# A gated product in two passes over its weights, with block pairs as the moved operand

## The chip, the cores and the metric

The kernel runs on one core of one Trainium2 chip, in one launch. The metric is the device time of the launch in microseconds, the median of several runs.

## The reference

```python
x = retention(q, k, v)                      # 4608 tokens x 512
h = x @ w_in                                # 512 -> 2048
g = h * cos(h)
x = g @ w_out                               # 2048 -> 512     (the stage that the change rewrites: "wo")
h = max(max(x @ w1, x @ w2), x @ w3)        # 512 -> 768      ("b")
out = h @ w_out2                            # 768 -> 512
```

## The kernel before

The 4608 tokens are 9 blocks of 512 (`NBLK`, `NB`); blocks 1 to 8 also make four pairs (`NDUO`), and block 0 stands alone. Every matrix product is cut into quarters and done with seven half-size products (`P_A11`, `P_A12`, `P_A22`, `P_S1` to `P_S4`), whose operands are quarters, differences and sums of differences of the quarters. Each operand is held as a high and a low part, so that a half-size product of one piece is three matmuls: low weight by high operand, high by high, high by low. The high part is a cast on ScalarE, the low part a subtraction on VectorE.

The stages follow each other on TensorE: attention, first gated product (`wi`, in two phases of nine blocks), second gated product (`wo`), the three products of `b`, the last product `o`. The order of the work is written by hand: TensorE's code advances a counter, one slot for the matmuls of one half-size product, and `at(n, fn)` puts `fn` (a cast, a difference, a load, a store) n slots later. Each engine does its instructions in the order in which they are written. DMAs are issued by SyncE (SP), in order too.

In `wo`, `phase_out` goes block by block; in a block, over 4 groups of two weight tiles; in a group, over the seven products, 12 matmuls of 256 moved columns each (`product_out`, L870). All eight weight tiles of `wo` are resident, and seven PSUM banks keep a block's sums over its 4 groups. `build_out` makes a group's operands: load of four quarters in two DMAs (`k_g<-gq`), four differences (L375, of which two operands `ta` and `tb` come), casts (L830, L838) and low parts (L834 for one quarter, L843 for pairs of 128x1024). `finish_out` adds the banks up and stores a block's result (`x2p<-o_wo`).

The gate `h*cos(h)` is done in `gate` (L510 to L523), and stored to `gq` in rows of 4 KB for each partition. Weights are prepared during earlier stages: `background` reads, converts and splits one weight tile of a later stage (L185 to L229; its sum on GpSimd is L196) and stores it; `take` loads such a tile whole (1792 KB); `take_split` loads the plain weights and splits them in place (L203 to L229). The weight tiles 4 to 7 of `wo` are split by `take_split` at the end of the first product and in the first 15 slots of `wo`.

Of the kernel before, what the change touches and what calls it, by code (L numbers as in the profile page):

```python
# [11 lines left out]
F32R = mybir.dt.float32r  # L12
# [8 lines left out]
NB = 512  # L21
# [80 lines left out]
def retention_ffn(ctx: ExitStack, tc: tile.TileContext, att, w_in, w_out, w123, w_out2, cst, out):  # L102
# [4 lines left out]
    xpool = ctx.enter_context(tc.tile_pool(name="xpool", bufs=22))  # L107
# [326 lines left out]
    def last_product(own_slot=True):  # L434

        g = pending.pop()
        if "last" in g:
            g["last"]()
            tick()
            return  # L440
        g["go"](g["d"], P_A22, False)
        nc.scalar.activation(g["s1"][:, 0], g["d"][:, : g["n"]], AF.Copy, scale=g["scale"])
        g["done"](g, 1)
        if own_slot:
            tick()

    def group_in(ws, xs, name, done, where, duo=False, tile=None, scale=1.0, seeded=None):
        n = NB if duo else HB * len(ws)
        g = {"name": name, "n": n, "done": done, "at": where, "scale": scale}
        tile = tile or x4  # L450

        def copy(dst, b):
            nc.scalar.activation(dst, b[:, :n], AF.Copy, scale=scale)  # L453

        def plus(dst, b):
            if scale == 1.0:
                nc.vector.tensor_tensor(out=dst, in0=dst, in1=b[:, :n], op=ALU.add)  # L457
            else:
                nc.vector.scalar_tensor_tensor(
                    out=dst, in0=b[:, :n], scalar=scale, in1=dst, op0=ALU.mult, op1=ALU.add  # L460
# [349 lines left out]
    for i, (n, m) in enumerate(((-13, -2), (-11, 0), (-9, 7), (-7, 12))):  # L810
        take_split("wo", 4 + i, endB + n, endB + n + 4, *(endB + m + k for k in (0, 1, 1, 2)))

    def gate_half(g, half):
        j, k = g["at"]
        gate(g[f"s{half}"], f"{g['name']}_{half}", gq[j][k][:, 2 * half : 2 * half + 2], 0 if half else 3)


    OUT_ORDER = (P_A11, P_A12, P_S4, P_S2, P_A22, P_S3, P_S1)

    def build_out(name, n, src, offs, load, t1=(0, nc.gpsimd), t3=(0, nc.gpsimd), last=3):  # L820

        o = {"name": name, "n": n}
        pairs = ((P_A12, P_S4, "k2"), (P_S2, P_A22, "tb"), (P_S1, P_S3, "ta"))

        def first_high():
            x = o["x"] = x4(f"x_{name}", [2, n], F32R)
            nc.scalar.copy(x[:, 0], o["k1"][:, 0])  # L830
            o[P_A11] = (x[:, 0], x[:, 1])

        def first_low():
            nc.vector.tensor_tensor(out=o["x"][:, 1], in0=o["k1"][:, 0], in1=f32(o["x"][:, 0]), op=ALU.subtract)  # L834

        def pair_high(k):
            h = o["h", k] = x4(f"h{k}_{name}", [2, n], F32R)
            nc.scalar.copy(h, o[pairs[k][2]])  # L838

        def pair_low(k):  # L840
            h = o["h", k]
            lo = x4(f"l{k}_{name}", [2, n], F32R)
            nc.vector.tensor_tensor(out=lo, in0=o[pairs[k][2]], in1=f32(h), op=ALU.subtract)  # L843
            for i in range(2):
                o[pairs[k][i]] = (h[:, i], lo[:, i])

        at(load, lambda: load_quarters(o, src))
        at(offs[t1[0]], lambda: difference(o, 1, t1[1]))
        at(offs[t3[0]], lambda: difference(o, 3, t3[1]))
        at(offs[0], first_high)  # L850
        at(offs[1], first_low)
        at(offs[1], lambda: pair_high(0))
        at(offs[2], lambda: difference(o, 2, nc.vector))
        at(offs[2], lambda: pair_low(0))
        at(offs[2], lambda: difference(o, 4, nc.vector))
        at(offs[3], lambda: pair_high(1))
        at(offs[last], lambda: pair_high(2))
        at(offs[4], lambda: pair_low(1))
        at(offs[5], lambda: pair_low(2))
        return o  # L860

    def product_out(b, ws, product, x, n, first, last):
        for mt in range(2):
            m = slice(mt * 128, mt * 128 + 128)
            for p, w in enumerate(ws):
                c = slice(p * HB, p * HB + HB)
                wh, wl = w[product][:, 0, m], w[product][:, 1, m]
                xh, xl = x[product][0][:, c], x[product][1][:, c]
                for i, (a, v) in enumerate(((wl, xh), (wh, xh), (wh, xl))):
                    nc.tensor.matmul(  # L870
                        b[:, mt * HB : (mt + 1) * HB],
                        a,
                        v,
                        start=first and mt == 0 and p == 0 and i == 0,
                        stop=last and p == len(ws) - 1 and i == 2,
                        skip_group_check=True,
                    )
# [533 lines left out]
```

## Time and profile before

| what | value |
| --- | --- |
| median of 3 runs | 1441.6 us (1440.66 to 1441.9) |
| the profiled execution's own time | 1442.28 us |
| its span in the trace | 1440.5 us |
| granted TensorE clock over the span | 0.995 |
| TensorE busy | 98% |
| VectorE / ScalarE / GpSimd busy | 81% / 54% / 12% |

The difference of 1.8 us between the time and the span lies outside what the trace shows. Busy shares are means over stages with different limits; for `wo` the windows of that stage count, which runs from 543.6 to 915.5 us.

### The profile page before, as it was taken

Reading aid. Unit: us, or ns where it says so; the run is one execution under the profiler, and the core shown is the slowest. Engines: PE = TensorE matmul, PEld = TensorE weight load, DVE = VectorE, ACT = ScalarE, POOL = GpSimd, SP = SyncE. Lnnn points to the kernel's source line nnn. Section 1 sums busy time; section 2 is a strip of 40 time slices with the busy share of each in tenths; the row PEclk is TensorE's granted clock in tenths of the full one; section 3 lists DMA queues with packets and bytes.
Section 4 is the critical chain, followed back from the end, with each engine's and each line's share of the span. In section 5 each row is a group of like instructions: output and inputs, shape, how many; then the busy total and the mean of one; then the engine's idle time right before and its main releaser. Section 6 shows DMA issues by size and latency. Waiting matters only on the chain.

```text
span 1440.5 us, 26312 instructions
## 1 busy us (share of the span) xinstructions
PE 1413.1 (98%) x10492; PEld 1299.3 (90%) x10492; DVE 1160.7 (81%) x1649; ACT 778.1 (54%) x1259; POOL 178.1 (12%) x128
## 2 busy tenths in 40 slices
PE   7999999999999998999999999999999999999998
PEld 5899999998999998999999999988888888888887
DVE  7988888779787779999999998668576667868875
ACT  4666666667787776444444443344344434534543
POOL 3343443331022000000000000000000000000000
PEclk9999999999999999999999999999999999999999
DMA  9779989868999985365565567723433294435633
GB/s 359 254 280 321 317 285 342 299 259 298 359 387 351 339 288 170 126 224 199 189 210 195 189 227 289 303 74 125 142 129 125 86 372 176 156 132 167 227 117 117
DMA packets 95034, 331.52 MB, mean 230 GB/s; under 512 B 9408, under 2 KB 17600, under 8 KB 88768
## 3 DMA queue, kind: packets, MB, share of 16 engines
q1 hardware_dynamic: 94912, 329.85, 64.4%
q8 instruction: 82, 1.34, 0.4%
q14 instruction: 40, 0.33, 0.1%
HBM read 197.69 MB, written 132.12 MB: 229 GB/s over the span
## 4 chain that ended last, share of the span: by engine, by line
PE 81%; DVE 3%; DMA 3%; issue 1%; ACT 0%; SPq 0%; DVEq 0%; ACTq 0%
PE wo L870 23%; PE d_e L428 13%; PE d_a L406 11%; PE b_e L428 7%; PE b_a L406 6%; PE d_u L1272 5%; PE a_e L428 3%; PE sums L406 3%; PE b_u L1272 2%; PE d_b L406 2%; PE sc L567 1%; PE po L626 1%; PE a_u L1272 1%; DMA k_z<-x2q 1%; PE state L610 1%; PE po L638 1%
## 5 line engine op out<-in xcount | busy, mean ns | idle before, releaser
L870 PE MATMUL wo<-h_g,w_wo 128*128 128x256 f32 x1728 | 313.3, 283 | 0.0
L870 PEld LDWEIGHTS wo<-h_g,w_wo 128*128 128x128 f32 x1728 | 269.9, 192 | 0.0
L870 PE MATMUL wo<-l_g,w_wo 128*128 128x256 f32 x864 | 245.4, 284 | 4.6 <-DVE l_g L843 4.5
L870 PEld LDWEIGHTS wo<-l_g,w_wo 128*128 128x128 f32 x864 | 166.1, 192 | 5.6 <-DVE l_g L843 5.4
L406 PE MATMUL d_a<-x_x,w_wi 128*128 128x256 f32 x864 | 122.5, 290 | 1.0 <-DVE x_x L383 1.0
L523 DVE SCALAR_TENSOR_TENSOR s_a<-t_a,s_a 128x1024 f32<-128x1024 f32 x72 | 93.6, 1300 | 31.1 <-ACT t_a L520 31.0
L428 PE MATMUL d_e<-h_e,w_b 128*128 128x512 f32 x432 | 115.5, 389 | 0.0
L406 PE MATMUL d_a<-x_y,w_wi 128*128 128x256 f32 x864 | 112.6, 287 | 2.5 <-DMA x_y<-xs 2.1
L406 PEld LDWEIGHTS d_a<-x_x,w_wi 128*128 128x128 f32 x864 | 108.3, 190 | 6.7 <-issue 1.9
L838 ACT CAST h_g<-tb_g 128x1024 fp32r<-128x1024 f32 x36 | 37.8, 1051 | 141.1 <-DVE tb_g L375 141.1
L406 PEld LDWEIGHTS d_a<-x_y,w_wi 128*128 128x128 f32 x864 | 108.9, 196 | 2.9 <-ACT ar_wo L184 2.3
L514 DVE SCALAR_TENSOR_TENSOR t_a<-s_a,t_a 128x1024 f32<-128x1024 f32 x72 | 96.0, 1334 | 18.0 <-ACT t_a L510 17.7
L453 ACT ACTIVATE ext<-d_e 128x512 f32<-128x512 f32 x72 | 43.0, 597 | 116.6 <-PE d_e L428 116.3
L428 PEld LDWEIGHTS d_e<-h_e,w_b 128*128 128x128 f32 x432 | 81.0, 188 | 16.8
L196 POOL TENSOR_TENSOR fa_b<-raw_b 128x512 uint32<-128x512 uint32 x18 | 22.5, 1250 | 537.5 <-DVE raw_b L190 506.8
L520 ACT ACTIVATE t_a<-t_a 128x1024 f32<-128x1024 f32 x72 | 76.0, 1055 | 21.9 <-DVE t_a L514 21.8
L594 ACT COPY u<-state 128x128 f32<-128x128 f32 x128 | 31.4, 264 | 96.6 <-PE state L610 96.2
L510 ACT ACTIVATE t_a<-s_a 128x1024 int32<-128x1024 f32 x72 | 76.1, 1056 | 1.3 <-PE d_a L406 0.4
L457 DVE TENSOR_TENSOR ext<-ext,b_e 128x512 f32<-128x512 f32 x36 | 24.7, 686 | 57.5 <-PE b_e L428 57.5
L428 PE MATMUL d_e<-l_e,w_b 128*128 128x512 f32 x216 | 66.5, 389 | 0.0
L406 PE MATMUL b_a<-x_x,w_wi 128*128 128x256 f32 x432 | 61.1, 289 | 0.6 <-DVE u L576 0.6
L406 PE MATMUL b_a<-x_y,w_wi 128*128 128x256 f32 x432 | 58.0, 283 | 1.7 <-DMA x_y<-xs 1.4
(268 smaller groups left out, 3248.4 us busy)
## 6 DMA issues: line engine op xcount, KB each, us to landing
u<-att SPq DMA_DIRECT2D x36, 1024.0 KB, 7.4
gq<-s_a SPq DMA_DIRECT2D x72, 512.0 KB, 5.4
k_g<-gq SPq DMA_DIRECT2D x72, 512.0 KB, 6.0
xs<-x_x SPq DMA_DIRECT2D x63, 512.0 KB, 5.5
x_y<-xs SPq DMA_DIRECT2D x63, 512.0 KB, 7.3
w_b<-st_b SPq DMA_DIRECT2D x9, 1792.0 KB, 11.3
st_b<-p_b SPq DMA_DIRECT2D x27, 512.0 KB, 5.1
mqp<-ext SPq DMA_DIRECT2D x24, 512.0 KB, 3.1
```

The source lines that it names most:

```text
L406: nc.tensor.matmul(h[:, p * HB : (p + 1) * HB], a, b, start=first and p == 0 and i == 0, stop=i == len(terms) - 1, skip_group_check=True,)
L428: nc.tensor.matmul(dst, a, b, start=first and i == 0, stop=i == len(terms) - 1, skip_group_check=True)
L453: nc.scalar.activation(dst, b[:, :n], AF.Copy, scale=scale)
L457: nc.vector.tensor_tensor(out=dst, in0=dst, in1=b[:, :n], op=ALU.add)
L510: nc.scalar.activation(st["t"], s, AF.Copy, bias=0.25)
L514: nc.vector.scalar_tensor_tensor(out=r, in0=s, scalar=MOST_TURNS, in1=st["t"], op0=ALU.min, op1=ALU.subtract)
L520: nc.scalar.activation(r, r, AF.Sin, scale=TURN, bias=HALF_PI)
L523: nc.vector.scalar_tensor_tensor(out=s, in0=f32(st["t"]), scalar=-1.0, in1=s, op0=ALU.max, op1=ALU.mult)
L594: nc.scalar.copy(um, st)
L838: nc.scalar.copy(h, o[pairs[k][2]])
L870: nc.tensor.matmul(b[:, mt * HB : (mt + 1) * HB], a, v, start=first and mt == 0 and p == 0 and i == 0, stop=last and p == len(ws) - 1 and ...
L1272: nc.tensor.matmul(dst, a, v, start=first and p == 0 and i == 0 and (wide or mt == 0), stop=p == 2 and i == 2, skip_group_check=True,)
```

## The change: two passes, block pairs, and accumulating DMAs

`wo` is done in two passes (`half`) over the weights: pass 0 with tiles 0 to 3, pass 1 with tiles 4 to 7. The unit of work is a block pair (`m` 0 to 3) or block 0 alone (`m` None). Pass 0 goes 0, None, 1, 2, 3, pass 1 goes None, 0, 1, 2, 3. A unit does the seven products over both groups of its half; a slot is 12 matmuls of one group and one product. A pair's matmul moves 512 columns as a view of 2 x 256; block 0's moves 256. `P_A22` of a unit is done inside the next unit, after its `P_S2` (`pending`).

A unit's operands are built from quarters of 128x1024 (`WO_STEPS`): seven casts, seven low parts, and three differences on VectorE for each group; the fourth, q0+q2, is formed by a DMA from GpSimd's queue that adds the quarter from DRAM onto the tile in SBUF (`add`). The gate is stored with its sign turned, into rows of 2 KB for each block of a pair (`gqp`). Results of pass 0 are stored plainly; those of pass 1 are added onto them in DRAM by accumulating DMAs from GpSimd's queue. `take_split` of tiles 4 to 7 goes to slots 34 to 65 of `wo`. Six backgrounds instead of seven run in `wo`, one more runs in the later stage of pairs. Tiles 2 to 5 of `b` are loaded product by product into the tiles 4 to 7 of `wo` as the last unit is done with them (`freed`). The pool `xpool` has 25 buffers instead of 22.

```diff
-    for i, (n, m) in enumerate(((-13, -2), (-11, 0), (-9, 7), (-7, 12))):
-        take_split("wo", 4 + i, endB + n, endB + n + 4, *(endB + m + k for k in (0, 1, 1, 2)))
...
+        dst = gqp[(j - 1) // 2][k][:, q, (j - 1) % 2] if j else gqs[k][:, q]
...
-    def product_out(b, ws, product, x, n, first, last):
-        for mt in range(2):
...
-                        b[:, mt * HB : (mt + 1) * HB],
...
+    WO_STEPS = (
+        (-6, "load", 0),
+        (-6, "load", 1),
+        (-5, "load", 3),
+        (-4, "load", 2),
+        (-2, "high", P_A11, 0),
+        (-1, "low", P_A11),
+        (-1, "less", 4, 1, 0, None),
+        (0, "high", P_S1, 4),
+        (1, "low", P_S1),
+        (2, "high", P_A12, 2),
+        (3, "low", P_A12),
+        (3, "less", 0, 3, 4, 0),
+        (4, "high", P_S2, 0),
+        (5, "low", P_S2),
+        (6, "add", 0, 2),
+        (8, "high", P_S4, 3),
+        (8, "less", 1, 3, 1, 1),
+        (9, "low", P_S4),
+        (10, "high", P_S3, 1),
+        (11, "low", P_S3),
+        (20, "high", P_A22, 0),
+        (21, "low", P_A22),
+    )
...
+        def add(i, d, q):
+            for k in sets[i]:
+                nc.gpsimd.dma_start(out=piece(ts[i][d], i, k), in_=src[k][:, q], accum_op=ALU.add)
...
+        def low(i, product):
+            h, t = ts[i]["high", product]
+            lo = x4(f"l{product}_{name}{i}", [2, NB], F32R)
+            nc.vector.tensor_tensor(out=lo, in0=t, in1=f32(h), op=ALU.subtract)
...
+        def go(banks, product, k, first):
+            hi, lo = ops[k][product]["hi"], ops[k][product]["lo"]
+            for mt in range(2):
+                c = slice(mt * 128, mt * 128 + 128)
+                to = banks[mt] if n == 2 else banks[0][:, mt * HB : (mt + 1) * HB]
+                to = to.rearrange("p (b n) -> p b n", b=n)
+                for p, w in enumerate(ws[k]):
+                    r = slice(p * HB, p * HB + HB)
+                    wh, wl = w[product][:, 0, c], w[product][:, 1, c]
+                    for i, (a, v) in enumerate(((wl, hi), (wh, hi), (wh, lo))):
+                        nc.tensor.matmul(
+                            to,
+                            a,
+                            v[:, :, r],
...
+        def both(banks, product, first=False):
+            go(banks, product, 0, first)
+            tick()
+            go(banks, product, 1, first)
...
+            if half:
+                nc.gpsimd.dma_start(out=dst[:, q], in_=t, accum_op=ALU.add)
+            else:
+                nc.sync.dma_start(out=dst[:, q], in_=t)
...
-    for i in range(7):
-        at(28 * i + 33, lambda: background(*back.pop(0), False))
...
+    for i in range(4):
+        t = 34 + 8 * i
+        take_split("wo", 4 + i, t, t + 3, t + 4, t + 5, t + 6, t + 7)
+    for i in range(6):
+        at((6, 24, 40, 76, 92, 110)[i], lambda: background(*back.pop(0), True, 2))
...
-    at(28 * (NBLK - 1) + 21, lambda: block_in(0, 0, 2, 3))
...
+    at(done_at - 6 - base, lambda: block_in(0, 0, 2, 3))
```

The order of the instructions moves in these places. On TensorE the first is the first group of `wo`; the right side of a name is the moved operand (`x` both parts of the first quarter, `h` high, `l` low) and the weight tile. Before, from the middle of the first product into the second:

```order
L870 MATMUL wo_0_6504<-x_g_0_6413,w_wo_4503 128x256 x3
L870 MATMUL wo_0_6504<-x_g_0_6413,w_wo_4883 128x256 x3
L870 MATMUL wo_1_6528<-h_g_0_6437,w_wo_4503 128x256 x2
L870 MATMUL wo_1_6528<-l_g_0_6455,w_wo_4503 128x256
L870 MATMUL wo_1_6528<-h_g_0_6437,w_wo_4883 128x256 x2
L870 MATMUL wo_1_6528<-l_g_0_6455,w_wo_4883 128x256
```

After the change the first unit's first product (`d`, two banks, one for each half of the output rows) stands as:

```order
L918 MATMUL d_g_0_6458<-h_g_00_6434,w_wo_4487 128x512 x2
L918 MATMUL d_g_0_6458<-l_g_00_6453,w_wo_4487 128x512
L918 MATMUL d_g_0_6458<-h_g_00_6434,w_wo_4867 128x512 x2
L918 MATMUL d_g_0_6458<-l_g_00_6453,w_wo_4867 128x512
L918 MATMUL d_g_0_6459<-h_g_00_6434,w_wo_4487 128x512 x2
```

A matmul now moves the columns of two blocks, and the third matmul of the stage already needs a low part `l`.

On VectorE the place is the same one in the program, the end of the last `wi` groups (`s_a` and `t_a` are the gate's) and the first operands of `wo`. Before (`s_wo`, `fa_wo` and `w_wo` are the splitting of the weight tiles 4 to 7):

```order
L523 SCALAR_TENSOR_TENSOR s_a_2_6249<-t_a_2_0_6396,s_a_2_6249 128x1024
L375 TENSOR_TENSOR tb_g_0_6453<-k_g_0_6372,ta_g_0_6434 128x512
L843 TENSOR_TENSOR l_g_0_6455<-k_g_0_6372,h_g_0_6437 128x1024
L375 TENSOR_TENSOR tb_g_0_6453<-tb_g_0_6453,k_g_0_6372 128x512
L459 SCALAR_TENSOR_TENSOR s_a_3_6367<-b_a_3_6374,s_a_3_6367 128x512
L203 TENSOR_TENSOR s_wo_6473<-fa_wo_6394 128x256
L204 TENSOR_TENSOR s_wo_6473<-s_wo_6473,fa_wo_6394 128x256
```

And with the change (`q_g` are the quarters, `q_g_00d` a difference):

```order
L459 SCALAR_TENSOR_TENSOR s_a_3_6340<-b_a_3_6343,s_a_3_6340 128x512
L514 SCALAR_TENSOR_TENSOR t_a_2_1_6419<-s_a_2_6249,t_a_2_1_6419 128x1024
L459 SCALAR_TENSOR_TENSOR s_a_3_6356<-d_a_3_6327,s_a_3_6356 128x512
L885 TENSOR_TENSOR l_g_00_6453<-q_g_00_6360,h_g_00_6434 128x1024
L865 TENSOR_TENSOR q_g_00d<-q_g_00_6362,q_g_00_6360 128x1024
L885 TENSOR_TENSOR l_g_01_6472<-q_g_01_6379,h_g_01_6451 128x1024
L865 TENSOR_TENSOR q_g_01d<-q_g_01_6381,q_g_01_6379 128x1024
L523 SCALAR_TENSOR_TENSOR s_a_2_6249<-t_a_2_1_6419,s_a_2_6249 128x1024
```

The weight splitting is gone from this place, and the first low part now stands behind two L459, the second of which reads the bank `d` of the last `wi` group.

GpSimd's queue held nothing but the sums L196 of the backgrounds in this stage. In the second pass it now holds the adding loads (L870 of the changed kernel), the adding stores (L950) and the sums:

```order
L870 DMA q_g_10_8026<-gqp_2_86 128x1024
L870 DMA q_g_11_8046<-gqp_3_87 128x1024
L950 DMA x2p_101<-o_g_1_8264 128x1024
L950 DMA x2q_100<-o_gs_8442 128x512
L196 TENSOR_TENSOR ar_b_8418<-ar_b_8418 128x512
L950 DMA x2p_101<-o_g_1_8388 128x1024
L950 DMA x2p_101<-o_g_1_8303 128x1024
```

The DMAs and the sums share one queue in order, and each of the DMAs stands behind a wait for the tile that it adds to or from.

## Rows read from the trace of the kernel before

**Rows 1.** The page's head: span, then busy time and share of each engine.
```profile
span 1440.5 us, 26312 instructions
...
PE 1413.1 (98%) x10492; PEld 1299.3 (90%) x10492; DVE 1160.7 (81%) x1649; ACT 778.1 (54%) x1259; POOL 178.1 (12%) x128
```

**Rows 2.** Windows: length, busy PE, PEld, DVE, ACT, POOL, clock, DMA share, GB/s.
```profile
545.00:600.00 55.00, 50.41 (x398) 49.30 (x397) 53.76 (x75) 30.95 (x43) 0.00 (x0) 0.97 0.42 145
600.00:650.00 50.00, 50.00 (x419) 50.00 (x418) 45.51 (x63) 23.89 (x31) 2.99 (x3) 1.00 0.59 201
...
1000.00:1100.00 100.00, 100.00 (x443) 82.78 (x442) 67.15 (x87) 41.66 (x68) 4.16 (x4) 1.00 0.34 116
...
440.00:460.00 20.00, 20.00 (x169) 20.00 (x168) 14.07 (x16) 15.69 (x23) 3.71 (x2) 1.00 1.03 390
```

**Rows 3.** Chain of waits, 440 to 1110 us: start, length, what.
```profile
566.86 328.26 PE wo L870 x2731
896.02 15.50 DMA k_z<-x2q
...
929.85 2.88 PE d_b L406 x24
...
1030.43 2.72 PE d_e L428 x12
```

**Rows 4.** TensorE's timeline at the start of wo: start, length, instruction, [idle before].
```profile
543.57 1.60 PE L870 MATMUL wo<-x_g,w_wo 128*128 128x256 f32 x12
...
551.62 0.39 PE L870 MATMUL wo<-l_g,w_wo 128*128 128x256 f32 x1 [3.00 <-DVE l_g L843]
...
552.83 0.63 PE L870 MATMUL wo<-h_g,w_wo 128*128 128x256 f32 x2
...
563.38 0.39 PE L870 MATMUL wo<-l_g,w_wo 128*128 128x256 f32 x1 [1.18 <-DVE l_g L843]
563.61 0.40 PE L870 MATMUL wo<-h_g,w_wo 128*128 128x256 f32 x2
```

**Rows 5.** TensorE's timeline at the end of wo.
```profile
915.34 0.28 PE L870 MATMUL wo<-l_g,w_wo 128*128 128x256 f32 x1
...
918.55 1.21 PE L406 MATMUL b_b<-x_z,w_b 128*128 128x256 f32 x8 [1.02 <-DVE x_z L383]
```

**Rows 6.** VectorE's timeline early in wo: start, length, instruction.
```profile
563.24 0.69 DVE L375 TENSOR_TENSOR tb_g<-tb_g,k_g 128x512 f32<-128x512 f32 x1
563.85 0.69 DVE L375 TENSOR_TENSOR ta_g<-k_g,k_g 128x512 f32<-128x512 f32 x1
564.45 1.22 DVE L514 SCALAR_TENSOR_TENSOR t_a<-s_a,t_a 128x1024 f32<-128x1024 f32 x1
565.58 1.22 DVE L843 TENSOR_TENSOR l_g<-tb_g,h_g 128x1024 fp32r<-128x1024 f32 x1
...
569.59 0.42 DVE L225 SCALAR_TENSOR_TENSOR w_wo<-fa_wo,w_wo 128x256 fp32r<-128x256 f32 x1
```

**Rows 7.** Groups by line, 545 to 916 us: busy, mean ns, idle before.
```profile
L870 PE MATMUL wo<-l_g,w_wo 128*128 128x256 f32 x864 | 245.4, 284 | 4.6 <-DVE l_g L843 4.5
...
L843 DVE TENSOR_TENSOR l_g<-ta_g,h_g 128x1024 fp32r<-128x1024 f32 x36 | 43.9, 1218 | 0.0
...
L838 ACT CAST h_g<-ta_g 128x1024 fp32r<-128x1024 f32 x36 | 37.6, 1046 | 0.8 <-DVE ta_g L375 0.8
...
L196 POOL TENSOR_TENSOR fa_b<-raw_b 128x512 uint32<-128x512 uint32 x14 | 18.3, 1310 | 374.0 <-DVE raw_b L190 343.4 <-ACT raw_b L185 30.7
```

**Rows 8.** DMA issues, 100 to 1000 us: KB each, median us to landing.
```profile
k_g<-gq SPq DMA_DIRECT2D x72, 512.0 KB, 6.0
gq<-s_a SPq DMA_DIRECT2D x69, 512.0 KB, 5.4
...
x2p<-o_wo SPq DMA_DIRECT2D x16, 512.0 KB, 4.0
...
k_z<-x2q SPq DMA_DIRECT2D x2, 512.0 KB, 15.7
```

More of the change, by code (lines that the diff above doesn't have):

```diff
@@ L809, in retention_ffn @@
     endB = endA + per * NBLK
-    for i, (n, m) in enumerate(((-13, -2), (-11, 0), (-9, 7), (-7, 12))):
-        take_split("wo", 4 + i, endB + n, endB + n + 4, *(endB + m + k for k in (0, 1, 1, 2)))
     def gate_half(g, half):
         j, k = g["at"]
[L815 to L860, printed above, removed]
@@ L907, in phase_out @@
-    def phase_out(kind, groups, todo, xs, scale, dsts):
-        for j, k in todo:
-            ws = [weights[kind, i] for i in groups[k]]
-            x = xs(j, k)
-            first, last = k == 0, k == len(groups) - 1
-            if first:
-                banks, f = {}, {}
-            for product in OUT_ORDER:
-                if first:
-                    banks[product] = bank(f"{kind}{j}_{product}")
-                if pending and product == P_A22:
-                    last_product(False)
-                product_out(banks[product], ws, product, x, HB * len(ws), first, last)
-                if last:
-                    finish_out(f, product, banks, scale, f"{kind}{j}", dsts[j])
-                tick()
@@ L924, in retention_ffn @@
-    outs = {}
-    x2_steps = {"t1": (1, nc.vector), "t3": (3, nc.vector), "last": 4}
-    def out_first():
-        outs[0, 0] = build_out("g0_0", NB, gq[0][0], range(2, 8), 0, **x2_steps)
+        q = slice(2 * half, 2 * half + 2)
+        dst = gqp[(j - 1) // 2][k][:, q, (j - 1) % 2] if j else gqs[k][:, q]
+        gate(g[f"s{half}"], f"{g['name']}_{half}", dst, 0 if half else 3)
+    WO_STEPS = (
[22 more added lines that the diff above has]
+    )
@@ new lines, in retention_ffn, with plan_wo @@
+    wo_order = [(half, m) for half, ms in enumerate(((0, None, 1, 2, 3), (None, 0, 1, 2, 3))) for m in ms]
+    base_of, pend_of, EARLY_OF = {}, {}, {}
+    wo_units = []
+    def plan_wo(base):
+        for i, key in enumerate(wo_order):
+            base_of[key] = base
+            pend_of[key] = 2 if i else 1
+            EARLY_OF[key] = 4 if i and wo_order[i - 1][1] is None else 0
+            base += 12 + pend_of[key]
+        for half, m in wo_order:
+            wo_units.append(wo_unit(m, half, base_of[half, m]))
+        return base
@@ L965, in block_in, with freed @@
         build_in(o, 0, (k1, k2, k2 + 1, k2 + 2), (k1, k1 + 2, k2, k2 + 2, k2 + 3, k2 + 4, k2 + 5), None, nc.vector)
-    at(28 * (NBLK - 1) + 21, lambda: block_in(0, 0, 2, 3))
-    phase_out("wo", [[2 * k, 2 * k + 1] for k in range(4)], todo, lambda j, k: outs.pop((j, k)), TURN * WSCALE**-2, x2q)
+    at(done_at - 6 - base, lambda: block_in(0, 0, 2, 3))
+    def freed(product):
+        for i in range(4):
+            w = weights["wo", 4 + i]
+            nc.sync.dma_start(out=f32(w[product]), in_=stash["b", 2 + i][:, product])
+            weights["b", 2 + i] = w
+    wo_units[-1]["freed"] = freed
+    for u in wo_units:
+        wo_group(u)
     free = []
@@ L1128, in retention_ffn @@
     for m in range(NDUO):
-        for n in (1,) if m < 3 else (1, 16):
+        for n in (1,) if m < 2 else (1, 16):
             at(n, lambda: background(*back.pop(0), False, 5))
```

182 lines of the change are left out of this document (123 added, 59 removed).

## The prediction

> **What bounds the kernel now.** I read the page's head first: TensorE is busy 98% of a span of 1440.5 us [rows 1], so time falls in two ways only: TensorE has less to do, or waits less. The chain of waits says the same of this stage: one piece of 328.26 us with 2731 matmuls of `wo` and nothing else in it [rows 3]. That is 120.2 ns for a matmul of 256 columns; 24 of them in another stage take 2.88 us, 120.0 ns. Then TensorE's timeline at both ends of `wo`. It begins at 543.57 [rows 4]; its last matmul starts at 915.34 and is followed 0.12 us later by the first of `b` [rows 5], so the stage takes 915.46 - 543.57 = 371.89 us. It holds 36 x 7 x 12 = 3024 matmuls and 12 of the last `wi` group (its `P_A22`): 3036 x 0.120 = 364.3 us. The other 7.6 us are lost at the start. 4.5 us are waits for low parts `l` from VectorE [rows 7], 3.00, 1.18 and a remainder [rows 4]; the other 3.1 are the clock: after the wait of 3.00 us a pair of matmuls takes 0.63 us where it takes 0.40 after the wait of 1.18 [rows 4], and the window there has a mean clock of 0.97 [rows 2]. Behind the end there is one wait of 1.02 us for `x_z`, whose quarters were late [rows 5]: that load took 15.50 us in the chain [rows 3].
>
> The windows show who is next. In the first 55 us VectorE is busy 53.76, then 45.51 of 50, 91% [rows 2], and TensorE does not wait there. ScalarE has half its time free.
>
> **The change, part by part.**
>
> *Twins.* Of 1680 matmuls 336 keep 256 columns and 1344 move 512 and stand for two each. A matmul of 512 columns, whose moved operand in the `b` stage has the same view of 2 x 256, takes 2.72 / 12 = 226.7 ns [rows 3]; two of 256 take 240.0. So 1344 x 13.3 ns = **-17.9 us**. The stage at full pace: 12 x 0.120 + 336 x 0.120 + 1344 x 0.2267 = 346.4 us.
>
> The Trainium skill ("TensorE: Matmul & The Clock Gate", section "Back-to-back issue gap") gives the gap of an isolated matmul on a warm clock as N/2.4 + 2.5 ns, that is 109.2 and 215.8 ns, by which a pair would save 2.6 ns and the term would be -3.5 us; the rows are 11 ns above both, and a saving of 13.3 is what this stream shows, so the measurement decides.
>
> *The start.* The splitting of weights 4 to 7 leaves VectorE's queue ahead of the first operands, so the 7.6 us go: **-7.6 us**. In their place the first low part (128x1024) stands behind the two L459 of the last `wi` group. The second of these needs that group's next to last product, which ends when TensorE is about to begin the unit. VectorE starts a 512-column instruction 0.60 us after the one before and a 1024-column one 1.13 us (563.24 to 564.45, 564.45 to 565.58), some 0.09 less than they last, so one of 256 some 0.34 [rows 6]: 0.60 + 1.13 + some 0.1 for the signals, less 0.45 us of the first two twin matmuls, is a wait of 1.4 us. A second one of 0.3 us or so may come where ScalarE copies the last `wi` bank ahead of a cast. The clock: after 1.18 us it held, after 3.00 it fell [rows 4]; a wait of 1.4 lies near the first. I take **+2.0 us**, with 0.5 and 5 (the clock falls, 3.1 us more) as ends.
>
> *The end.* `block_in` is asked 6 slots of 2.72 us ahead, 16.3 us, not 7 of 1.44, 10.1. The loads landed in 15.5 to 15.7 us [rows 3, 8], beside whole tiles of `b`, which are now loaded elsewhere or in pieces. The wait of 1.02 goes: **-1.0 us**, with 0 as the other end.
>
> *VectorE.* For a unit of a pair: 3 differences and 7 low parts for each of two groups, 20 x 1.13, and 6 additions from banks at 0.60: 26.2 us against 168 x 0.2267 = 38.1 of TensorE. Block 0: 10 x 1.13 + 3 x 0.60 = 13.1 against 20.2. The first pass has four pairs and block 0 (117.9), three backgrounds (5.4 each), four splittings (3.5 each: four sums and a low part of 256 columns, three low parts of 512; a background has two more of each) and what is left of the gate (5 x 1.13): 153.8 us against some 168 on TensorE, 91%. That is the share at which it kept up before [rows 2]. The fullest unit has its 26.2 and some 11 more, 37.5 of 38.1: if instructions took their whole 1.22 instead of 1.13 it would be over by some 3 us. The second pass has 134 of 172, 78%. ScalarE has 14 casts of 1.05 [rows 7] and 8 copies of some 0.6 in a pair's unit, 19.5 of 38.1. The background moved to the later pair stage meets a VectorE that is 67% busy [rows 2]: nothing.
>
> *The fourth difference.* It leaves VectorE for a DMA, asked in slot 6 of a unit and needed by the cast in slot 20: 14 x 2.72 = 38 us ahead, where a plain load of the same 512 KB lands in 6.0 us [rows 8]. An accumulating DMA is nowhere in the trace. Its bounds: as a plain one, 0; or late, see the rivals. Each stands on GpSimd behind at most two sums of 1.3 us [rows 7], since the queue is in order. I take 0.
>
> *Traffic.* Twice the reading of 9.4 MB of differences and two passes of results raise the stage from some 79 MB to 100 (119 if an addition counts twice), over 349 us 285 to 340 GB/s. A full window moved 390 [rows 2], so it fits on the mean; stretches can fill up. Rows of 2 KB instead of 4 cost nothing that shows: results in 2 KB rows landed in 4.0 us, the gate's 4 KB rows in 5.4 [rows 8]. The gate's stores (36 of 0.5 MB in the second `wi` phase, where the DMA share is 1.03 [rows 2]) could grow by some per cent, 4 us at most, but x loads are asked a block, some 20 us, ahead: 0 to +4, taken with the allowance.
>
> *Allowance.* For small waits in ten units whose order is new (casts behind copies, buffers not free): **+3.0 us**, ends 0 and 12.
>
> **Sum.** 1442.28 - 17.9 - 7.6 + 2.0 - 1.0 + 3.0 = 1420.8 us for an execution like the profiled one. That one is 0.7 us above the median of the runs, so 1420.1, **1420 us**. About 0.2% (2.9 us) is what a measurement of this kernel can tell from no change.
>
> **The rivals.**
>
> A. *VectorE or a DMA queue becomes the bound in the first pass.* For it: 91%, one unit at 37.5 of 38.1, and an order without slack where several steps hang on one cast. Against it: the same share before, with no TensorE wait after 567 us [rows 2, 3]. Price: the overrun of 3 us in one to three units, and for each wait as long as 3 us another 3 us of lower clock [rows 4]: +4 to +16 on the sum without the allowance's middle, **1424 to 1436 us**. Chance 0.20.
>
> B. *The additions land late; the kernel is slower.* The cast before `P_A22` waits, ScalarE's queue waits behind it, then VectorE's low part and TensorE. Of 10 units 9 have such a place inside the stage. The gain is 21.5 us, so this decides from 21.5 / 9 = 2.4 us lost at each, a landing of some 40 us. For it: no row prices an addition, and it reads its target and its source; the stores of the second pass share the queue. Against it: 40 us is nearly seven times the 6.0 of a plain load. At 4 us each the time is 1420 + 36 = **1456 us**. Chance 0.08.
>
> The Trainium skill ("SBUF — State Buffer", section "Who interferes with whom") says that a DMA issued from GpSimd can be held up while VectorE works in a two-port mode, since GpSimd writes its descriptors over the shared port, and that subtractions of two tensors have no such mode; the nearest row here agrees in kind, GpSimd's sum taking 1.31 us beside a VectorE that is nine tenths busy [rows 2, 7], but no DMA from GpSimd is in this trace, so the chance above does not rest on the page.
>
> C. *The twins give nothing.* If 512 columns cost 2 x 120.0 ns here, as weights of one tile are now used in another sequence, the 17.9 us stay away: **1438 us**. Against it stands the same view at 226.7 [rows 3]. Chance 0.05. By the skill's gap the time would be 1420 + 17.9 - 3.5 = 1434 us, inside this case.
>
> **How the numbers follow.** The forecast has 0.67, with a range of its own of 1415 to 1424: the start's and the allowance's lower ends give 1420.1 - 1.5 - 3 = 1415.6, the start's upper end 1423. A 0.20, C 0.05, B 0.08. The range of 8 in 10 begins just below, at 1414.5, and reaches into A to 1432, which leaves out B, C and the upper third of A. Faster by over 0.2% means under 1438.7: the forecast, A but for a tail of 0.02, and 0.03 of C, 0.88. The same: those tails, 0.04. Slower: B, 0.08.
>
> **What would show it.** In the trace after: matmuls of L918 with 512 columns 227 ns apart; `wo` some 350 us from its first matmul to the first of `b`; at its start one wait of 1 to 2 us for L885 with the clock held; no wait for `x_z` at its end. VectorE some 90% busy in the first pass and 80% in the second, and idle time ahead of L918 below 5 us in all. The additions landing in under 20 us. Wrong would be: waits ahead of L918 in every unit, released by VectorE (A) or, by way of ScalarE's cast, by a DMA (B); twin matmuls 240 ns apart (C); a granted clock below 0.97 in the stage; or waits in the second `wi` phase for `x_y`, from the gate's shorter rows.

## The result, and the profile after

The changed kernel takes 1448.9 us (median of 6 runs, 1446.6 to 1450.2) where the kernel before took 1441.3 in the same session: ratio 1.0055, 95% interval 1.0044 to 1.0065. The forecast was 1420 with a range to 1432, so it was wrong by 28.8 us and on the wrong side of no change.

The page's head and its table of DMA queues (packets, MB, share of 16 engines) answer to [rows 1]. The span is 1445.5 us. TensorE has 11 us less to do than before and yet ends later. A queue that did not exist before, the one of the DMAs that GpSimd issues (q0), has 18.9 MB.

```profile
span 1445.5 us, 23684 instructions
...
PE 1402.3 (97%) x9148; PEld 1229.4 (85%) x9148; DVE 1123.0 (78%) x1532; ACT 807.2 (56%) x1304; POOL 211.9 (15%) x168
...
q1 hardware_dynamic: 105952, 329.85, 63.5%
q0 software_dynamic: 5760, 18.88, 7.2%
```

TensorE's timeline answers to [rows 4, 5]. It shows the borders of the stages (first `d_g`, the first `d_gs` of the second pass, first `d_b`, first `d_e`, first `d_u`) and the larger waits in brackets.

```profile
542.15 0.73 PE L918 MATMUL d_g<-h_g,w_wo 128*128 128x512 f32 x2
544.52 0.50 PE L918 MATMUL d_g<-l_g,w_wo 128*128 128x512 f32 x1 [1.64 <-DVE l_g L885]
...
603.90 0.39 PE L918 MATMUL d_gs<-l_gs,w_wo 128*128 128x256 f32 x1 [2.17 <-DVE l_gs L885]
...
684.17 0.62 PE L918 MATMUL d_g<-h_g,w_wo 128*128 128x512 f32 x2
...
687.57 0.62 PE L918 MATMUL b_g<-h_g,w_wo 128*128 128x512 f32 x2
...
720.25 0.40 PE L918 MATMUL d_gs<-h_gs,w_wo 128*128 128x256 f32 x2
...
743.59 0.39 PE L918 MATMUL d_gs<-l_gs,w_wo 128*128 128x256 f32 x1 [3.10 <-DVE l_gs L885]
...
757.01 0.51 PE L918 MATMUL b_g<-l_g,w_wo 128*128 128x512 f32 x1 [1.28 <-DVE l_g L885]
...
779.24 0.69 PE L918 MATMUL b_g<-l_g,w_wo 128*128 128x512 f32 x1 [2.67 <-DVE l_g L885]
...
903.78 0.50 PE L918 MATMUL d_g<-l_g,w_wo 128*128 128x512 f32 x1 [2.30 <-DVE l_g L885]
...
908.92 1.60 PE L406 MATMUL d_b<-x_z,w_b 128*128 128x256 f32 x12
...
943.18 1.09 PE L428 MATMUL d_e<-h_e,w_b 128*128 128x512 f32 x4
...
1124.95 2.07 PE L428 MATMUL d_e<-h_e,w_wo 128*128 128x512 f32 x4 [3.00 <-DVE ext L457]
...
1309.56 0.63 PE L1363 MATMUL d_u<-h_u,w_o 128*128 128x512 f32 x2
```

The twins are as cheap as forecast: from 684.17 to 687.57 lie 15 matmuls, 226.7 ns each. What is lost is between them. In the kernel before, the stage of pairs had these borders:

```profile
945.52 1.09 PE L428 MATMUL d_e<-h_e,w_b 128*128 128x512 f32 x4
...
1304.22 0.63 PE L1272 MATMUL d_u<-h_u,w_o 128*128 128x512 f32 x2
```

The table gives the stages by such borders. "Full pace" is the number of matmuls times 120.0 or 226.7 ns; the first pass holds 12 matmuls of the last `wi` group, and the `P_A22` of each pass's last unit (5.4 us) is done in what follows the pass.

| stretch | full pace | changed kernel | lost |
| --- | --- | --- | --- |
| first pass, 542.15 to 720.25 | 168.5 | 178.1 | 9.6 |
| second pass, 720.25 to 908.92 | 172.5 | 188.7 | 16.2 |
| stage of pairs, 943.18 to 1309.56 | 358.7 (kernel before) | 366.4 | 7.7 |

33.5 us are lost, of which the forecast had 5.0 (the start and the allowance); 28.5 are to be explained. This execution took 1447.3 us, 26.5 more than the 1420.8 of the sum: the other 2.0 come back outside these stretches, 1.4 of them ahead of `wo`, which begins at 542.15 instead of 543.57 [rows 4]. (On the medians the error is 28.8, 2.3 larger, since the profiled execution of the changed kernel was 1.6 us faster than its median and that of the kernel before 0.7 slower.) So three places are to be explained, and the second pass first.

The windows of the two passes (columns as in [rows 2]) say that VectorE is not short: it is busy 90% of the first pass, as forecast, and 74% of the slower second. DMA engines are busy 91% of the second pass, with 263 GB/s, where a full window of the kernel before moved 390 [rows 2].

```profile
545.00:720.00 175.00, 171.04 (x825) 143.36 (x824) 158.16 (x188) 103.96 (x141) 17.65 (x16) 0.99 0.78 251
720.00:905.00 185.00, 173.23 (x825) 143.82 (x824) 137.25 (x151) 92.14 (x123) 31.38 (x33) 0.99 0.91 263
```

The timelines of ScalarE and VectorE name what they wait for. Behind each of these rows stands a wait of TensorE.

```profile
740.04 1.22 DVE L885 TENSOR_TENSOR l_g<-q_g,h_g 128x1024 fp32r<-128x1024 f32 x1 [5.74 <-DMA x2q<-o_gs]
...
777.96 1.23 DVE L885 TENSOR_TENSOR l_g<-q_g,h_g 128x1024 fp32r<-128x1024 f32 x1 [5.45 <-DMA x2p<-o_g]
...
901.90 0.69 DVE L375 TENSOR_TENSOR ta_z<-k_z 128x512 f32<-128x512 f32 x1 [8.30 <-DMA k_z<-x2q]
...
741.02 0.67 ACT L184 ACTIVATE ar_b<-ar_b 128x512 f32<-128x512 f32 x1 [6.58 <-DMA ar_b<-w]
...
752.78 0.66 ACT L184 ACTIVATE ar_b<-ar_b 128x512 f32<-128x512 f32 x1 [8.64 <-DMA ar_b<-w]
...
832.04 1.05 ACT L878 CAST h_g<-q_g_11d 128x1024 fp32r<-128x1024 f32 x1 [6.17 <-DMA st_b<-p_b]
...
861.63 1.09 ACT L941 ACTIVATE o_g<-d_g 128x512 f32<-128x512 f32 x2 [8.73 <-DMA x2p<-o_g]
```

All end with a DMA, and of three kinds. A raw weight tile (`ar_b<-w`) is there too late, with the casts of the operands queued behind its conversion. Its first half is asked two slots ahead. Its second half goes into the same buffer, so its load is not issued before GpSimd's sum has read the first half. For the wait that ends at 752.78 the sum ran until 748.15 and the load went out at 748.18; it landed after 4.5 us, and was late by its issue:

```profile
747.11 1.04 POOL L196 TENSOR_TENSOR ar_b<-ar_b 128x512 uint32<-128x512 uint32 x1 [16.17 <-DVE ar_b L190]
...
748.18 0.33 SPq L178 DMA_DIRECT2D ar_b<-w  x1
```

A store (`x2p`, `x2q`, `st_b`) has not landed when a new operand needs its tile. The first load of the next stage (`k_z`) is late, with a low part of `wo` queued behind it.

TensorE's waits in the second pass add up to 11.8 us. The granted clock adds little to them, and the length of a wait does not say whether it falls: behind the wait of 3.10 us at 743.59 it stayed at full speed, behind that of 2.67 at 779.24 its mean over 5 us was 0.66, which costs 1.7 us.

```profile
743.50:748.00 4.50, 4.41 (x30) 4.11 (x31) 4.47 (x8) 0.65 (x1) 0.89 (x1) 1.00 1.01 430
779.00:784.00 5.00, 4.76 (x14) 3.81 (x15) 3.48 (x5) 1.15 (x3) 0.00 (x0) 0.66 1.05 362
```

The DMAs of 720 to 905 us (median us to landing in the last column) show how late things have become; [rows 8] answers to it.

```profile
q1 hardware_dynamic: 10938, 36.44, 54.6%
q0 software_dynamic: 3744, 12.06, 36.1%
...
q_g<-gqp SPq DMA_DIRECT2D x32, 512.0 KB, 9.1
x2p<-o_g POOLq DMA_DIRECT2D x13, 512.0 KB, 9.1
...
st_b<-p_b SPq DMA_DIRECT2D x9, 512.0 KB, 11.6
q_g<-gqp POOLq DMA_DIRECT2D x8, 512.0 KB, 9.2
```

The kernel before, in the same window:

```profile
k_g<-gq SPq DMA_DIRECT2D x36, 512.0 KB, 6.1
...
st_b<-p_b SPq DMA_DIRECT2D x12, 512.0 KB, 4.2
```

The adding DMAs of q0 take 36.1% of the engines' time for 12.06 MB, the plain ones 54.6% for 36.44: twice the time for a byte. And everything lands later, the plain stores `st_b` after 11.6 us instead of 4.2.

### The profile page after: what moved, and what is told of

It is laid out like the page before. It is cut to its first block, busy times and chain, and to the rows that moved or that the text cites. A ratio compares the mean times of both kernels' runs of the same rounds, so it can differ in the third digit from the quotient of the medians.

```text
span 1445.5 us, 23684 instructions
## 1 busy us (share of the span) xinstructions
PE 1402.3 (97%) x9148; PEld 1229.4 (85%) x9148; DVE 1123.0 (78%) x1532; ACT 807.2 (56%) x1304; POOL 211.9 (15%) x168
## 5 line engine op out<-in xcount | busy, mean ns | idle before, releaser
L918 PE MATMUL d_g<-h_g,w_wo 128*128 128x512 f32 x512 | 158.7, 391 | 0.1
L885 DVE TENSOR_TENSOR l_g<-q_g,h_g 128x1024 fp32r<-128x1024 f32 x96 | 116.9, 1227 | 28.2 <-ACT h_g L878 14.9
L918 PEld LDWEIGHTS d_g<-h_g,w_wo 128*128 128x128 f32 x512 | 95.9, 189 | 20.2 <-ACT h_g L878 0.8
L878 ACT CAST h_g<-q_g 128x1024 fp32r<-128x1024 f32 x96 | 98.5, 1047 | 23.3 <-DVE q_g L865 15.0
L918 PE MATMUL d_g<-l_g,w_wo 128*128 128x512 f32 x256 | 100.4, 392 | 5.6 <-DVE l_g L885 5.6
L918 PE MATMUL b_g<-h_g,w_wo 128*128 128x512 f32 x256 | 80.4, 396 | 0.3 <-ACT h_g L878 0.3
L428 PE MATMUL d_e<-h_e,w_wo 128*128 128x512 f32 x256 | 69.6, 394 | 4.4 <-DVE ext L457 3.0
L918 PEld LDWEIGHTS d_g<-l_g,w_wo 128*128 128x128 f32 x256 | 48.2, 188 | 17.7 <-DVE l_g L885 7.8
L428 PEld LDWEIGHTS d_e<-h_e,w_wo 128*128 128x128 f32 x256 | 48.4, 190 | 15.2 <-DVE ext L457 3.4
```

The costliest lines, as they stand in the source:

```text
L428: nc.tensor.matmul(dst, a, b, start=first and i == 0, stop=i == len(terms) - 1, skip_group_check=True)
L878: nc.scalar.copy(h, ts[i][q])
L885: nc.vector.tensor_tensor(out=lo, in0=t, in1=f32(h), op=ALU.subtract)
L918: nc.tensor.matmul(to, a, v[:, :, r], start=first and k == 0 and p == 0 and i == 0 and (n == 2 or mt == 0), stop=k == 1 and p == 1 and i == 2,
```

## The experiments

Times are medians; ratios are to the kernel before, run on the same chip in the same session (1440.4 to 1441.5 us), with the 95% interval. The changed kernel was run in one session alone, so differences from it compare sessions. Pass times are from one profile each, and the profiled execution lies up to 4.4 us off its kernel's median: differences of two or three us between passes are not firm.

**Adding stores.** `e1_plain_stores`:

```diff
-            if half:
-                nc.gpsimd.dma_start(out=dst[:, q], in_=t, accum_op=ALU.add)
-            else:
-                nc.sync.dma_start(out=dst[:, q], in_=t)
+            nc.sync.dma_start(out=dst[:, q], in_=t)
```

> The results of the second pass are stored plainly from SP's queue instead of being added by DMAs from GpSimd's queue; the sum of the two passes is left out. Theory 1, tiles held by the adding stores: in the trace after, an adding store lands 9.1 us after its issue and a plain one 3.8, and VectorE and ScalarE wait there for tiles that such a store holds (5.7, 5.5, 8.7, 2.1 us); without them the waits of TensorE at 743, 779, 834 and 865 us go, 7.3 us and the clock that falls behind 779 (some 2), so 1438 to 1442 us. Theory 2, raw weights asked too late (ScalarE waits 28.6 us for them): no change, 1446 to 1450, since the loads stay where they are.

1437.3 us (0.9972, 0.9962 to 0.9982), 11.6 less than the changed kernel; second pass 178.2, first unchanged at 178.2. The waits at 743, 779, 834 and 865 us are gone; ScalarE still waits 23.1 us for raw weights. So the adding stores cost 10.5 us of the second pass as against plain ones. The edit also changes the queue that issues them, and it leaves out the sum of the two passes.

**Raw weights asked earlier.** `e2_loads_early` (lag 5, both halves at once; the sixth begins three slots earlier so that its stores precede the loads that read them):

```diff
-        at((6, 24, 40, 76, 92, 110)[i], lambda: background(*back.pop(0), True, 2))
+        at((6, 24, 40, 76, 92, 107)[i], lambda: background(*back.pop(0), True, 5, True, 5))
```

> The six weight preparations of this stage ask for both halves of a raw tile five slots (13.6 us, 7.2 in the units of 256 columns) ahead of the conversion, not two. Theory 2: ScalarE's 28.6 us of waiting for raw weights go, and with them TensorE's waits at 755 to 757 us and most of those that stand behind them, some 5 to 9 us of the time: 1440 to 1444. Theory 1, tiles held by the adding stores: ScalarE's waits go, but TensorE's stay, 1446 to 1450.

1433.2 us (0.9946, 0.9927 to 0.9964), 15.7 less, more than either theory had. ScalarE's waits for raw weights fall from 28.6 to 3.3 us; first pass 173.7, second 182.7. TensorE's waits at 779, 834 and 865, which had been put down to stores, are gone as well; those at the start and the end of the second pass stay (3.41 us at 741, 2.01 at 894). So the causes are not separate; a late conversion makes what is queued behind it late, stores and operands too. The edit does two things: it asks earlier, and it gives the second half a buffer of its own, so that its load no longer waits for GpSimd's sum. No run tells these two apart.

**The fourth operand on VectorE.** `e3_sum_on_vector`:

```diff
-            for k in sets[i]:
-                nc.gpsimd.dma_start(out=piece(ts[i][d], i, k), in_=src[k][:, q], accum_op=ALU.add)
+            nc.vector.tensor_tensor(out=ts[i][d], in0=ts[i][d], in1=ts[i][q], op=ALU.add)
```

> The fourth operand q0+q2 is formed by an addition of 128x1024 on VectorE instead of an adding load from GpSimd's queue: 18 additions of 1.13 us, 20.3 us more for VectorE, 9.4 MB less in and out of memory, and nothing ahead of the adding stores in GpSimd's queue but the sums. Theory 3, VectorE is the bound: slower by 5 to 15 us, 1454 to 1464, mostly in the first pass. Theory 1 or 2, the waits are for DMAs: within 3 us of the changed kernel, or faster where the adding stores now land earlier, 1442 to 1450.

1437.6 us (0.9978, 0.9966 to 0.9991), 11.4 less, with 20 us more work on VectorE. First pass 179.7 (1.6 more), second 181.7 (7.0 less), in an execution that was 3.9 us above the median. VectorE as the bound of the whole falls; the adding loads cost more than the sums that they replace. DMAs of the second pass:

```profile
q0 software_dynamic: 2447, 7.87, 25.7%
...
q_g<-gqp SPq DMA_DIRECT2D x32, 512.0 KB, 6.5
...
st_b<-p_b SPq DMA_DIRECT2D x9, 512.0 KB, 9.0
```

Plain loads land in 6.5 us instead of 9.1, stores in 9.0 instead of 11.6. `k_z`, asked as before, lands in 7.9 instead of 10.7, and the wait of 2.30 us at the end of the second pass is gone.

**The preparation put back.** `e4_one_back`:

```diff
-        at((6, 24, 40, 76, 92, 110)[i], lambda: background(*back.pop(0), True, 2))
+        at((6, 24, 40, 76, 92, 110, 124)[i], lambda: background(*back.pop(0), True, 2))
...
-        for n in (1,) if m < 2 else (1, 16):
+        for n in (1,) if m < 3 else (1, 16):
```

> The seventh weight preparation goes back from the later pair stage into the second gated product, near its end (slot 124). Theory 4: in the trace after the pair stage has 4.8 us of new TensorE waits around 1105 and 1125 us and 6.8 us at the lower clock behind them (3.4 us lost), because VectorE has two preparations at once there; undone, 8 us come back: 1440 to 1443. Rival: the preparation costs as much in the last unit of the second pass, where VectorE and the store queues are as full: 1446 to 1451.

1442.9 us (1.0021, 1.0010 to 1.0032), 6.0 less. The stage of pairs takes 357.9 us, as before the change, and the second pass 3.0 more. Over all profiles, the stage takes 363.2 to 367.1 us in the nine kernels that have the preparation there and 357.9 to 358.5 in the five that put it back. So the moved preparation cost 5 to 9 us there. The timelines of VectorE and ScalarE of the changed kernel show how:

```profile
1101.66 1.23 DVE L1164 TENSOR_TENSOR r_e<-r_e,r_e 128x1024 f32<-128x1024 f32 x1 [3.58 <-DMA st_b<-p_b]
...
1103.61 0.66 ACT L184 ACTIVATE spare<-raw_o 128x512 f32<-128x512 f32 x1 [2.65 <-DMA raw_o<-w_out]
...
1124.40 0.60 ACT L453 ACTIVATE ext<-b_e 128x512 f32<-128x512 f32 x1 [5.04 <-DVE ext L1078]
```

A tile waits for a store, a conversion for its raw weights, and VectorE, which then has two preparations at once, makes ScalarE wait 5.04 us for the merge that frees its target; TensorE waits 3.00 us at 1124.95 and goes on at half the clock for the next 5 us. The same wait was 3.27 us in the profile of `e7_copies` and 3.28 in that of `e13_adds_unread`; the mean clock of the 5.1 us behind it was 0.70 in the one and 1.00 in the other, which is part of the spread.

**Two at once.** `e5_early_one_back` has the edits of e2 and e4 (slots 6, 24, 40, 76, 92, 107, 124).

> The early loads of raw weights and the preparation put back (slot 124) together. Theory: the two losses lie in different stages and add up. From the changed kernel's 1448.9 the first gave -15.7 and the second -6.0: 1427, with the pair stage at 358 us as in the kernel before. Rival: the preparation put back fills the last unit, whose DMA engines are full, and gives part of the gain back: 1431 to 1435.

1430.3 us (0.9922, 0.9905 to 0.9939): between the two. Stage of pairs 358.3, second pass 183.1. At the end of the second pass TensorE waits 2.79 us behind the late `k_z`.

**All four.** `e6_all` adds the sum of e3, and

```diff
-    at(done_at - 6 - base, lambda: block_in(0, 0, 2, 3))
+    at(done_at - 10 - base, lambda: block_in(0, 0, 6, 7))
```

> Early raw loads, the preparation put back, the fourth operand summed on VectorE and the first loads of the next stage asked four slots earlier. Theory 5, the DMA engines are full in the second pass and whatever takes bytes from them or asks earlier helps: 1418 to 1426, near the sum made before the change (1420), TensorE's waits in the stage under 6 us. Theory 3, with the DMA waits gone VectorE is the bound in the first pass (153.8 + 9 of 168 us): 1428 to 1436, with the waits there released by VectorE that never waits itself.

1428.8 us (0.9912, 0.9893 to 0.9932), where theory 3 had it. Second pass 175.8 with no wait at its end. That this is due to the earlier asking of `k_z` is not shown: in `e3_sum_on_vector`, without the adding loads, that wait was gone with the old asking. But the first pass is 177.8 instead of 173.8 in e5: there, with VectorE busy 168.7 of 175 us, the sums do cost time.

**Bytes or additions.** `e7_copies` is e3 and

```diff
+            for k in sets[i]:
+                nc.gpsimd.dma_start(out=dram(f"no{q}_{name}_{k}", [n, NB] if n == 2 else [NB]), in_=src[k][:, q])
```

> The sum is on VectorE as in e3_sum_on_vector, and each adding load is replaced by a plain copy of the same bytes within DRAM, from GpSimd's queue at the same place; nothing reads the copies. Theory 5, the DMA engines' time is what counts: the second pass takes again 186 to 190 us (181.7 without the copies, 188.7 in the changed kernel), the whole 1443 to 1450. Theory 6, the adding load itself counts, by its landing or the tile that it holds: no change from e3_sum_on_vector, 1436 to 1439.

1438.6 us (0.9981, 0.9971 to 0.9991): 1.1 us more than e3, inside the intervals; second pass 178.1, in the fastest of the ten executions. The same number of bytes in the same queue, moved plainly, costs nothing that can be told, though the DMA engines are busy 90% again. Theory 5 falls as it was put: the busy share alone does not decide.

**Where the adding loads stand.** `e9_adds_later`:

```diff
-        (6, "add", 0, 2),
         (8, "high", P_S4, 3),
         (8, "less", 1, 3, 1, 1),
         (9, "low", P_S4),
+        (9, "add", 0, 2),
```

> The adding loads stand three slots (8.2 us) later in GpSimd's queue, behind the adding store of a unit's first quarter instead of ahead of it; nothing else moves. Theory 7, an adding store lands late because the two adding loads of the unit are ahead of it in the one queue (issued 1 to 4 us before it, landings of 10 to 11 us where plain stores take 3.8): that store lands sooner, VectorE and ScalarE wait less for its tile, and the second pass goes from 188.7 to 180 to 185 us, the whole to 1440 to 1445. Theory 6, the adding loads cost what they cost wherever they stand: 1446 to 1450.

1453.9 us (1.0099, 1.0077 to 1.0121): 5 slower, which neither theory had; second pass 195.8. The wait at 779 is gone, but others come: ScalarE waits 33.4 us for raw weights, and plain stores land still later. Issued in one burst with the store, the adding loads take 13.1 us:

```profile
st_b<-p_b SPq DMA_DIRECT2D x9, 512.0 KB, 14.3
...
q_g<-gqp POOLq DMA_DIRECT2D x8, 512.0 KB, 13.1
```

**Sums on VectorE in the second pass alone.** `e10_hybrid` is e6 with

```diff
+            if half:
+                nc.vector.tensor_tensor(out=ts[i][d], in0=ts[i][d], in1=ts[i][q], op=ALU.add)
+                return
+            for k in sets[i]:
+                nc.gpsimd.dma_start(out=piece(ts[i][d], i, k), in_=src[k][:, q], accum_op=ALU.add)
```

> As e6_all, but with the sum on VectorE in the second pass alone; the first pass keeps its adding loads, where no adding store shares the queue. First pass 173 to 175 us as in e5_early_one_back (173.8, against 177.8 with the sums on VectorE), second 175 to 177 as in e6_all: 1423 to 1427. Rival: the first pass is slow for another reason than VectorE's sums, and the time is that of e6_all, 1428 to 1431.

1424.7 us (0.9888, 0.9871 to 0.9904), as expected: first pass 173.8, second 176.4, stage of pairs 358.5. It beats both kernels, the one before by 16 us. Its borders:

```profile
544.43 0.73 PE L921 MATMUL d_g<-h_g,w_wo 128*128 128x512 f32 x2
...
718.20 0.40 PE L921 MATMUL d_gs<-h_gs,w_wo 128*128 128x256 f32 x2
...
894.57 1.59 PE L406 MATMUL d_b<-x_z,w_b 128*128 128x256 f32 x12
```

**The twins undone.** `e11_halves` is e10 with each matmul of 512 columns as two of 256:

```diff
-                        nc.tensor.matmul(
-                            to,
-                            a,
-                            v[:, :, r],
+                        for h in range(n):
+                            nc.tensor.matmul(
+                                to[:, h],
+                                a,
+                                v[:, h, r],
```

> As e10_hybrid, but each matmul of 512 columns is two of 256 with the same weights. Theory 8, the term of the twins is right, 1344 x 13.3 ns: 17.9 us slower than e10_hybrid, less what the small waits there give back (up to 5): 1437 to 1444, matmuls 120 ns apart. Rival, the twins save little here: within 5 us of e10_hybrid.

1435.2 us (0.9964, 0.9952 to 0.9976), 10.5 more than e10, and so between the theories. From 821.39 to 828.60 lie 60 matmuls, 120.2 ns each, so the term of 17.9 us is there:

```profile
821.39 0.64 PE L922 MATMUL d_g<-h_g,w_wo 128*128 128x256 f32 x4
...
828.60 0.64 PE L922 MATMUL d_g<-h_g,w_wo 128*128 128x256 f32 x4
```

The passes take 179.8 and 182.0 us, 3.3 in all over the full pace of 256 columns (177.1 and 181.4); e10's take 173.8 and 176.4, 9.2 over its own. About 6 us of the twins' gain are given back as waits; the operands must come faster there.

**One tile less.** `e12_tiles24`:

```diff
-    xpool = ctx.enter_context(tc.tile_pool(name="xpool", bufs=25))
+    xpool = ctx.enter_context(tc.tile_pool(name="xpool", bufs=24))
```

> The changed kernel with 24 tiles in the pool of operands, not 25; nothing else. Theory 1, the pool comes round to tiles whose stores have not landed: with one tile less every such wait starts sooner, and the whole is 3 to 10 us slower, 1452 to 1459, with more waits of VectorE and ScalarE for x2p, x2q and st_b stores. Rival: waits of that kind only mark what was late anyway, and one tile is neither here nor there, 1446 to 1451.

1450.0 us (1.0051, 1.0032 to 1.0069): not to be told from the changed kernel. That is the rival's range and below theory 1's; but the five executions spread from 1445.7 to 1454.5, so theory 1 is made unlikely and not ruled out.

**Additions that nobody reads.** `e13_adds_unread` is e3 and

```diff
+            for k in sets[i]:
+                nc.gpsimd.dma_start(out=src[k][:, d], in_=src[k][:, q], accum_op=ALU.add)
```

> The sum is on VectorE as in e3_sum_on_vector, and each adding load is replaced by an adding DMA of the same bytes within DRAM, onto a quarter of the gate that has been loaded already; nothing reads it afterwards. Theory 9, an adding transfer holds up the others (plain loads landed in 9.1 us in the changed kernel, 6.5 with the sums on VectorE, 7.0 with plain copies): the second pass is 186 to 190 us again and the whole 1444 to 1450. Theory 10, it is only an adding load into a tile of the pool that costs, by what waits for that tile: as e3_sum_on_vector, 1436 to 1440.

1445.1 us (1.0029, 1.0019 to 1.0038): 7.6 of the 11.4 us of e3 are lost again, to adding transfers that hold no tile and that nothing waits for. The second pass takes 183.8 us, less than the 186 to 190 that theory 9 had. With e7 this shows for the loads that the addition costs, where a plain transfer of the same bytes costs next to nothing. The copies delay others too, but less: plain loads land in 6.5 us in e3, 7.0 with the copies, 8.0 with the additions. What the other 3.8 us are was not separated. The DMAs of 720 to 905 us, e7 first, then e13 (`no_g` and `gqp<-gqp` are the transfers in question):

```profile
q0 software_dynamic: 3739, 12.58, 33.9%
...
q_g<-gqp SPq DMA_DIRECT2D x32, 512.0 KB, 7.0
...
no_g<-gqp POOLq DMA_DIRECT2D x8, 512.0 KB, 6.5
```

```profile
q0 software_dynamic: 3457, 11.54, 36.6%
...
q_g<-gqp SPq DMA_DIRECT2D x32, 512.0 KB, 8.0
...
gqp<-gqp POOLq DMA_DIRECT2D x8, 512.0 KB, 9.7
```

**Plain stores, and additions beside them.** `e14_plain_and_adds` is e1 and

```diff
+            if half:
+                g, to = ((0, 0), (0, 1), (1, 0), (0, 3))[q]
+                x = (gqs if m is None else gqp[m])[2 * half + g]
+                nc.gpsimd.dma_start(out=x[:, to], in_=x[:, 2], accum_op=ALU.add)
```

> The results of the second pass are stored plainly from SP's queue, as in e1_plain_stores (the sum of the passes is left out), and in the place of each adding store GpSimd's queue has an adding DMA of the same bytes within DRAM, onto quarters of the gate that have been loaded; nothing waits for it. Theory 9, adding transfers hold up the other transfers: the 11.6 us that plain stores gave are lost again, 1444 to 1450, the second pass 185 to 190 us. Theory 1, what costs is the tile that an adding store holds until it has landed: as e1_plain_stores, 1435 to 1440, the second pass 178 to 181.

1471.8 us (1.0217, 1.0200 to 1.0234), far over either; second pass 214.4. Waiting for nothing, the additions go out in bursts of up to five, beside stores that the other kernels did not have on top; `k_z` lands after 24.8 us and TensorE waits 16.3 for what stands behind it. Against `e1_plain_stores`, which lacks only these additions, that is 34.5 us. It shows that additions without any held tile can do all the harm, and more, but not how the 11.6 us of the adding stores divide between the held tile, the queue and the traffic. That stays open, and so does whether adding stores issued two slots earlier would cost less: `e8_stores_early` gave no time.

## Why the prediction was wrong

The terms for work held; the waits that were put at nothing did not. Four steps failed: the weight preparations counted by VectorE's time alone, the fourth difference at 0 and the traffic that "fits on the mean", the moved preparation at "nothing", and the end at -1.0.

*What bounds the kernel, and the twins.* Right. 226.7 ns, 17.9 us less matmul time; but the sum took it as won whole, and e11 shows 10.5 of it. The isolated gap of the Trainium skill ("TensorE: Matmul & The Clock Gate", section "Back-to-back issue gap") would have made it some 3.4 us by estimate (the prediction rounds it to 3.5). The rows of the changed kernel disagree again, with 11 ns over that gap.

*The start.* Right: 1.64 us for the first low part, clock held, where 1.4 was forecast, and 1.10 later; the weights' splitting no longer stands there. The reading of the old start was off: 3.1 us were put down to the clock as what was left, while its mean of 0.97 over 55 us [rows 2] makes 1.7.

*VectorE.* Right as a budget: 158.2 of 175 us in the first pass, where 91% was forecast. But a budget says nothing of what an engine waits for in order, and that is where the time went. What failed is the counting of a weight preparation as 5.4 us of VectorE. It also has a conversion on ScalarE, queued ahead of the operands' casts. That waits for a load asked two slots ahead (2.9 us in the units of 256 columns, 5.4 in the others) where such a load landed in 4.7 to 6.4 us, or for the load of the second half, which waits in its turn for GpSimd's sum. The diff showed the lag of 2 in place of 3. ScalarE waits 28.6 us for raw weights; asked earlier and into two buffers, 25.3 of these go and 15.7 us of the time come back (e2).

*The fourth difference and traffic.* "I take 0" failed, but not as rival B had it. The adding loads land in 9.2 us, far within the 38, and no cast waited long for them. They make other transfers late (e13). So, as it seems, do the adding stores: without them plain loads land in 7.9 us instead of 9.1 (e1). "It fits on the mean" failed: the engines were 91% busy at 263 GB/s. Adding transfers take twice the engines' time of plain ones for a byte, and the second pass has 10 adding loads and 20 adding stores beside the preparations' loads and stores. The price was 11.4 and 11.6 us, each taken alone (e3, e1). They are not to be added to the 15.7 of e2: the sum, 38.7, is more than the 25.8 that both passes lose, as would be if each edit loosens the same chain.

*The moved preparation.* "Nothing", by a VectorE that is 67% busy on the mean [rows 2], failed: 7.7 us in that stage, which e4 gives back there, with 6.0 for the whole. The mean over 100 us hid a stretch of some 30 us in which two preparations, one behind the other, meet the operands of a new pair.

*The end.* The wait of 1.02 us for `x_z` went, but the late `k_z` now stands in VectorE's queue ahead of a low part of `wo`, and TensorE waits 2.30 us for that. With fewer adding transfers (e3) the wait is none, and none with four slots more besides (e6).

*The rivals.* Case A, waits made by VectorE or a DMA queue, was the right kind, in the wrong pass and priced at 4 to 16 us instead of 20.8 over what the sum had allowed (25.8 less 5.0), with no price for what a moved preparation does elsewhere. Its 1424 to 1436 also has the allowance's 3 us in, which its words leave out; without them it is 1421 to 1433. And its price for the clock, 3 us for each wait as long as 3, is not borne out: the wait of 3.10 us at 743.59 cost no clock, that of 2.67 at 779.24 cost 1.7. C was wrong: the twins are 226.7 ns apart, not 240.

The mechanism of the change is sound: with both passes, the pairs and the adding stores kept, and four edits around them, e10 takes 1424.7 us, 4.6 above the forecast.

## What to carry to other kernels

Cost a moved piece of work by each queue in which its instructions stand, and by what each of them waits for: a load's lead in slots is to be multiplied by the shortest slot that it will meet, and a load into a buffer that is still being read has no lead at all. Take an accumulating DMA as two transfers, and look at what else must land in that stretch, not at its own lead alone. When TensorE's work shrinks, every lead given in slots shrinks with it, and the gain shows only as far as the operands keep up.

## What was not expected of the hardware

An adding DMA takes 5.5 us of all sixteen engines for a MB (36.1% of 185 us for 12.06 MB), a plain one 2.8 (54.6% for 36.44): twice. The queue alone does not do it: e7's plain copies add 4.71 MB and 8.2% to what q0 holds in e3, some 3.2 us for a MB. An adding DMA of 512 KB lands in 9.1 to 9.7 us where a plain copy from the same queue lands in 6.5 (e7). The Trainium skill ("DMA: Bandwidth & Descriptors", section "Anatomy of one DMA — SWDGE (gpsimd) path") fits 2.0 us and the bytes at 436 GB/s, 3.2 us for this size by estimate. The median landings here are two to three times that, and they decide. At equal busy shares (0.90) the adding transfers cost 7.6 us and the plain ones 1.1 (e13, e7); why is not shown.
